# Loads on a second queue, a later transform back and moved weight splits in a one-core kernel: state-space convolution, then an MLP mixer

## The chip, the cores and the metric

The kernel runs on one core of one Trainium2 chip. The metric is the device time of one execution in microseconds (us), the median of three runs. A core has TensorE (PE, products), VectorE (DVE), ScalarE (ACT), GpSimd (Pool) and SyncE (SP). DMAs are issued from SP, ACT or Pool; each of the three has its own queue.

## The reference

Inputs are in fp32; L = 2048 rows, D = 512 channels.

```python
x = A_u
mod = (_silu(c) @ w_mod).reshape(c.shape[0], 6, 1, -1)
sa, ca, ga, sb, cb, gb = ...
h = _layernorm(x) * (1 + ca) + sa
x = x + ga * A_ref(h, ...)       # state-space convolution along L
h = _layernorm(x) * (1 + cb) + sb
x = x + gb * B_ref(h, ...)       # mixer
# A_ref: K[d, l] = Re sum_n C[d,n] exp(dt*A[d,n]*l) dt*B[d,n], l = 0..2047
#        y = irfft(rfft(u, 4096) * rfft(K, 4096))[:2048] + u * Dskip
# B_ref: h  = gelu(layernorm(x) @ w1); its four channel quarters shifted by +1, -1, +2, -2 rows
#        x1 = x + shifted(h) @ w2
#        out = x1 + gelu(layernorm(x1) @ w3) @ w4      # w3 is 512 x 1376
```

## The kernel before, in words

The order on each engine is the order in which the code is written, inside blocks of `tc.manual_schedule()`; tiles come from pools, and a framework puts in the waits. An engine and a DMA queue run their line strictly in order: what stands behind a waiting instruction waits too.

The work has five stages.

1. Up to about 209 us: the convolution kernel K is built (exponentials, sines, products), the normalised input is taken through a first transform and stored to DRAM as VU. During this stage Pool copies w3, w4 and w2 to DRAM scratch (`WD`), in pieces hung on the steps of that loop (`side`).
2. `k_first`: eight rounds of products turn K (tile KX) into VK0 and VK1, one for each half `jh` of 256 channels.
3. Sixteen steps, two halves `jh` of eight `kc`. A step takes the block of VU loaded by `load_vu` (512 KB, a tile of the pool `ldp`, name `ld`), transforms it (`spectrum_u`, ACT copies it to `us`), transforms K (`spectrum_k`), multiplies both on DVE (`multiply`: four products `ma`, `mb` and two sums `zc`), and in the next step transforms back (`back`: PE to PSUM `pz`, ACT copies to `z`, Pool stores z to DRAM as ZT in two DMAs of 256 KB). On ACT, z of the step before stands ahead of `us` of the step after. `flip` makes a sign-changed copy T3 of a part of table T2 on Pool. Table `Gm` belongs to `back`, table `FI` to the inverse.
4. The inverse: `load_inv(jh, k)` reads ZT back (512 KB or halves of it), `inv_half` multiplies with FI on PE, and DVE adds the result to x, which lies in X2, the same memory as KX (`load_x`, four loads of 1 MB). For the first half `jh = 0` the groups g = 0, 3, 1, 2 of four row tiles run during or right after the steps, with `half_stat` on DVE for the statistics; for the second half they run after the gap in which the last z makes its way through DRAM.
5. Mixing and channel groups. Mixing takes the eight tiles t = 7, 0, 1, 2, 3, 4, 5, 6 of 256 rows: modulation and statistics on DVE, normalisation on ACT (`mix_norm`), transposes on PE, then `mix_half(t, hl, hf)`: products with w1, a gelu on ACT into tile `go` (two buffers), and `mix_out` stores `go` to DRAM (GD). Tiles 4 to 6 are mixed inside the channel groups. A channel group g reads four shifted windows of GD (`chan_load`), multiplies with w2 (`chan_sum`), normalises, and runs w3, gelu and w4 (`chan`).

All products of the mixer are in three parts: a value is split into a high part (ACT rounds it to fp32r) and a low part (DVE subtracts), for weights and for the moving data (`nh`, `nl`). `weights` makes the tiles of one weight and a `load` that returns a function `split`. `split_w(n)` runs the next n splits of w3 and w4, each of 512 columns by 128 rows, in the order in which they were loaded.

Of the kernel before, what the change touches and what calls it, by code (L numbers as in the profile page):

```python
# [106 lines left out]
def body(ctx, tc, A):  # L107
# [11 lines left out]
    GD = dpool.tile([4, 128, 20, 128], F32, name="GD")  # L119
    WD = {k: dpool.tile(list(A[k].shape), F32, name="D" + k) for k in ("w2", "w3", "w4")}  # L120

# [425 lines left out]
    with tc.manual_schedule():  # L547
# [49 lines left out]
        for f in later:  # L597
# [8 lines left out]
    TU = TU[0]  # L606
    Gm = c2.tile([128, 2, 64], F32, name="Gm")
# [47 lines left out]

    t3s = {}

    def flip(kc):
        t = t3s[kc] = c2.tile([128, 8, 64], F32, name="T3", bufs=3)
        for gh in range(2):  # L660
            r = slice(gh * 64, gh * 64 + 64)
            P.tensor_scalar(t[r], T2[kc // 4][r, kc % 4 * 4:kc % 4 * 4 + 8, 64 - gh * 64:128 - gh * 64], -1.0, None, op0=OP.mult)

    def spectrum_k(jh, kc):
        p = [kbank([128, 2, 2, 128]) for gh in range(2)]
        for i in range(2):
            for ro in range(2):
                for ri in range(2):
                    for kk in range(2):
                        for gh in range(2):  # L670
                            k1 = kc * 4 + 2 * kk + i
                            rows = slice(gh * 64, gh * 64 + 64)
                            w = T2[k1 // 16][rows, k1 % 16]
                            if ri == gh:
                                w = w[:, ro * 64:ro * 64 + 64]
                            elif ro == ri:
                                w = w[:, gh * 64:gh * 64 + 64]
                            else:
                                w = t3s[kc // 2 * 2][rows, k1 % 8]
                            T.matmul(p[gh][kk * 64:kk * 64 + 64, i, ro], w,  # L680
                                     VK[jh][rows, ri * 32 + k1].rearrange("p j g -> p (j g)"),
                                     start=(ri == 0), stop=(ri == 1), skip_group_check=True)
        return p
# [33 lines left out]
    def load_inv(jh, k, i=None, q=Y):  # L717
        if (jh, k) not in zis:
            zis[jh, k] = block()
# [23 lines left out]
    def weights(pl, src, rows, cols, name, ntile):  # L743
        hi = pl.tile([128, ntile, cols], F32R, name=name + "h")
        lo = pl.tile([128, ntile, cols], F32R, name=name + "l")

        def load(stage, i, m=1, c0=0, c1=cols):
            n = min(128, rows - i * 128)
            w = stage(m, c1 - c0) if stage else lo.bitcast(F32)[:, i:i + m, c0:c1]
            Y.dma_start(w[:n], src[i * 128:i * 128 + (m - 1) * 128 + n, c0:c1].rearrange("(a p) n -> p a n", p=n))  # L750

            def split():
                for j in range(m):
                    h = hi[:n, i + j, c0:c1]
                    act(h, w[:n, j])
                    V.tensor_sub(lo[:n, i + j, c0:c1], w[:n, j], h.bitcast(F32))  # L756
            return split
        return hi, lo, load

    def two(m, n):  # L760
        return block().rearrange("p (a c) b -> p a (c b)", a=2)

# [79 lines left out]

    def mix_w(hl, f2):
        p = psw.tile([128, 2, 256], F32, name="pm")
        for e in range(2):
            three(p[:, e], W1h, W1l, hl, slice((f2 * 2 + e) * 128, (f2 * 2 + e + 1) * 128))
        return p

    def mix_out(g, hf, go):
        Y.dma_start(dram(GD, (2 + 2 * g) * 128 + hf * 256 * 2560, [[2560, 128], [128 * 2560, 2], [1, 256]]), go)  # L850
        if g not in (0, 7):
# [76 lines left out]

    def mix_half(t, hl, hf):
        p = mix_w(hl, hf)  # L930
        go = gop.tile([128, 2, 256], F32, name="go")
        act(go, p, AF.Gelu_apprx_tanh)
        mix_out(t, hf, go)
# [148 lines left out]
    splits = []  # L1082
# [9 lines left out]
    def split_w(n):  # L1092
        for _ in range(n):
            splits.pop(0)()

    steps = [(jh, kc) for jh in range(2) for kc in range(8)]
    with tc.manual_schedule():
        load_vu(*steps[0])
        flip(0)
        Y.dma_start(Gm, A["G"].rearrange("p (a b) -> p a b", a=2))  # L1100
        for r in range(8):
            k_first(r)
            if r == 3:
                load_vu(*steps[1])
            if r == 6:
                load_vu(*steps[2])
        us = spectrum_u(*steps[0])
        split = None
        for n, st in enumerate(steps):
            p = spectrum_k(*st)  # L1110
            multiply(*st, us, p)
            if n == 7:
                v0x.close()
                pw2 = ctx.enter_context(pool("pw2", side="right", reuse_waits="tile"))
                pw1 = ctx.enter_context(pool("pw1", side="right", reuse_waits="tile"))
                W2h, W2l, ldw2 = weights(pw2, WD["w2"], 512, 512, "w2", 4)
                W1h, W1l, ldw1 = weights(pw1, A["w1"], 512, 512, "w1", 4)
            if n > 0:
                back(*steps[n - 1])
            if n == 15:  # L1120
                i1 = inverse_parts(0, 1, psb, "pk2")
# [8 lines left out]
            if n == 9:  # L1130
                Y.dma_start(FI, A["FI"].rearrange("p (a b c) -> p a b c", a=32, b=2))
            if split:
                split()
                split = None
            if n in (8, 9):
                split = ldw1(two, n % 2 * 2, 2)
            if n == 10:
                for k in (0, 3, 4, 7):
                    load_inv(0, k)
            if n == 12:  # L1140
                inverse(0, 0)
                w2s = [ldw2(None, 2 * i, 2) for i in range(2)]
                for b in range(4):
                    half_stat(b, 0)
            if n == 13:
                inverse(0, 3)
                for k in (1, 2, 5, 6):
                    load_inv(0, k)
            if n in (14, 15):
                w2s.pop()()  # L1150
        for f in i1:
            f()
        back(*steps[15])
        s2x.close()
        tp = lambda name, bufs=1, **k: pool(name, bufs, reuse_waits="tile", **k)
        cm = ctx.enter_context(tp("cm", 2, side="right"))
        hv = ctx.enter_context(tp("hv", side="right"))
        gop = ctx.enter_context(tp("gop", 2, side="right"))
        psT = ctx.enter_context(tp("psT", space=PSUM))
        psw = ctx.enter_context(tp("psw", 2, space=PSUM))  # L1160
# [6 lines left out]
        for k, i in ((3, 1), (0, 0)):  # L1167
            load_inv(1, k, i, Y)
            load_inv(1, k + 4, i, S)
        for k, i in ((3, 0), (0, 1)):  # L1170
            load_inv(1, k, i)
            load_inv(1, k + 4, i)
        for i in range(2):
            inv_half(0, 2, i, psy, "py")()
        for b in (14, 15, 4, 5, 6, 7):
            half_stat(b, 0)
        for k in (1, 2):
            load_inv(1, k)
            load_inv(1, k + 4)
        keep(6)  # L1180
        inv_half(1, 3, 1, psy, "py")()
# [48 lines left out]
        load_w3(0)  # L1230
        mix_half(1, hl, 0)
        mix_norm(2)
        first_stats(3)
# [10 lines left out]
        load_w4(2)  # L1244
        mix_half(2, hl, 0)
        chan_split(0)
        mix_norm(3)
# [6 lines left out]
        add1 = chan_sum(0, 1)  # L1254
        split_w(1)
        n = cm.tile([128, 2, 512], F32, name="h2")
# [9 lines left out]
        stat0(0)  # L1266
        split_w(1)
        add1()
        mix_half(3, hl, 0)
        stat0(1)  # L1270
        norm0(0)
        norm0(1)
        split_w(1)
        mix_half(3, hl, 1)
        r = transposed(n)
        split_w(1)
        r = parts_of(r)
        split_w(4)
        chan_add(0)
# [22 lines left out]
```

## Time and profile before

| | us |
|---|---|
| median of three runs (689.29 to 690.67) | 690.18 |
| the profiled execution | 691.26 |
| its span, first to last instruction | 689.5 |

Mean granted TensorE clock 0.989. In the profile an instruction is named by its line, its engine, what it writes and what it reads (`zc<-ma`). `L115` is the helper `act`, through which all of ACT's copies and functions go. In a row of the timeline stand the start, the duration and, in brackets, the idle time ahead of it and who ended it. Rows of the waits read: engine, tile and line that waited, `<-` who was waited for, total us, times, longest.

### The profile page before, as it was taken

How to read it: one execution, taken by the hardware profiler on the slowest of the kernel's cores; microseconds unless marked ns; L12 is line 12 of the kernel's file. 1: busy time of each engine (PE TensorE's matmuls, PEld its weight loads, DVE VectorE, ACT ScalarE, POOL GpSimd, SP SyncE). 2: the span in 40 equal slices, each digit the busy share in tenths (PEclk: the TensorE clock that was granted, in tenths of full speed). 3: DMA queues.
4: the chain of work that ended last, by engine and by line, in shares of the span. 5: the costliest groups of instructions: out<-in, count | busy, mean ns of one | idle time of the engine just before them, and what ended most of it. 6: DMA issues, size and time to landing. Idle time of an engine off the chain costs nothing.

```text
span 689.5 us, 16884 instructions
## 1 busy us (share of the span) xinstructions
PE 642.6 (93%) x7195; PEld 509.2 (74%) x7195; DVE 498.0 (72%) x795; ACT 331.2 (48%) x505; POOL 124.8 (18%) x236
## 2 busy tenths in 40 slices
PE   1899999999999998977998999999999999999996
PEld 0456655655569776634887889999899889898895
DVE  7899999999996887986987967464574536363522
ACT  3878988889875557432444623123131312222121
POOL 4011112112103355413741101001010000000000
PEclk9999999999999999998999999999999999999999
DMA  8603264643739997967387010020100201010001
GB/s 299 284 2 79 75 218 105 209 121 85 275 85 317 354 335 258 346 204 226 108 257 240 1 32 32 16 77 15 47 31 17 77 1 62 1 49 13 1 31 31
DMA packets 51091, 86.42 MB, mean 125 GB/s; under 512 B 4676, under 2 KB 39496, under 8 KB 48424
## 3 DMA queue, kind: packets, MB, share of 16 engines
q1 hardware_dynamic: 46712, 66.74, 30.1%
q0 software_dynamic: 3440, 17.57, 7.4%
q8 instruction: 56, 0.92, 0.6%
q10 hardware_dynamic: 864, 1.05, 0.5%
q14 instruction: 19, 0.16, 0.1%
HBM read 59.12 MB, written 32.90 MB: 133 GB/s over the span
## 4 chain that ended last, share of the span: by engine, by line
PE 70%; DVE 6%; DMA 5%; ACT 3%; POOL 2%; issue 1%; ACTq 0%; SPq 0%; DVEq 0%; POOLq 0%
PE pm L841 7%; PE pm L838 7%; PE pm L839 7%; PE xx L448 7%; PE pa L954 6%; PE pa L955 6%; PE pa L962 6%; PE kp L498 3%; DMA ZT<-z 3%; PE ph L893 2%; PE ph L895 2%; PE ph L892 2%; DMA ld<-ZT 2%; PE pu L426 2%; PE pT L803 2%; PE pk L626 2%
## 5 line engine op out<-in xcount | busy, mean ns | idle before, releaser
L115 ACT ACTIVATE gh<-pm 128x512 fp32r<-128x512 f32 (+1 forms) x48 | 26.9, 560 | 200.7 <-PE pm L841 200.7
L838 PE MATMUL pm<-nh,w3h 128*128 128x256 f32 (+1 forms) x352 | 86.6, 281 | 2.7 <-ACT nh L115 2.7
L839 PE MATMUL pm<-nh,w3l 128*128 128x256 f32 (+1 forms) x352 | 86.3, 280 | 0.1
L946 DVE TENSOR_TENSOR gl<-gf,gh 128x512 fp32r<-128x512 f32 (+1 forms) x48 | 30.8, 643 | 68.4 <-ACT gf L115 68.4
L954 PE MATMUL pa<-w4h,gh 128*128 128x512 f32 (+1 forms) x176 | 69.6, 395 | 0.0
L838 PEld LDWEIGHTS pm<-nh,w3h 128*128 128x128 f32 (+1 forms) x352 | 66.0, 187 | 4.4 <-ACT nh L115 2.9
L955 PE MATMUL pa<-w4l,gh 128*128 128x512 f32 (+1 forms) x176 | 68.9, 392 | 0.0
L839 PEld LDWEIGHTS pm<-nh,w3l 128*128 128x128 f32 (+1 forms) x352 | 65.9, 187 | 2.2 <-DVE w3l L756 0.5
L765 POOL TENSOR_TENSOR rs<-mv,eps_t 128x1 f32<-128x1 f32 (+1 forms) x39 | 11.0, 282 | 282.4 <-DVE mv L771 265.4
L841 PE MATMUL pm<-nl,w3h 128*128 128x256 f32 (+1 forms) x352 | 55.0, 278 | 0.0
L449 PE MATMUL xx<-MG,ON 64*128 64x512 f32 x160 | 48.1, 397 | 0.0
L962 PE MATMUL pa<-w4h,gl 128*128 128x512 f32 (+1 forms) x176 | 48.0, 390 | 0.0
L448 PE MATMUL xx<-MG,ON 64*128 64x512 f32 x160 | 48.0, 396 | 0.0
L841 PEld LDWEIGHTS pm<-nl,w3h 128*128 128x128 f32 (+1 forms) x352 | 47.0, 187 | 0.0
L898 DVE TENSOR_TENSOR h<-h,ph 128x512 f32<-128x512 f32 x16 | 11.0, 687 | 45.1 <-PE ph L895 45.1
L466 DVE SCALAR_TENSOR_TENSOR e<-tr,p 128x512 f32<-128x512 f32 x64 | 41.1, 684 | 1.5 <-ACT tr L115 1.5
L498 PEld LDWEIGHTS kp<-e,e 128*32 128x32 f32 x2048 | 30.1, 110 | 12.7 <-issue 7.6
L475 DVE TENSOR_TENSOR e<-tr,p 128x1024 f32<-128x1024 f32 x32 | 39.0, 1220 | 0.0
L476 DVE TENSOR_TENSOR e<-tr,m 128x1024 f32<-128x1024 f32 x32 | 39.0, 1219 | 0.0
L115 ACT ACTIVATE p<-xx 128x1024 f32<-128x1024 f32 (+1 forms) x40 | 37.5, 979 | 2.2 <-PE xx L252 1.0
L962 PEld LDWEIGHTS pa<-w4h,gl 128*128 128x128 f32 (+1 forms) x176 | 33.0, 188 | 7.3 <-DVE gl L946 0.2
L115 ACT ACTIVATE tr<-xx 128x1024 f32<-128x1024 f32 x32 | 33.0, 1030 | 9.6 <-PE xx L449 7.9
(236 smaller groups left out, 1731.6 us busy)
## 6 DMA issues: line engine op xcount, KB each, us to landing
VU<-vs SPq DMA_DIRECT2D x64, 128.0 KB, 3.7
ld<-VU SPq DMA_DIRECT2D x16, 512.0 KB, 7.4
ZT<-z POOLq DMA_DIRECT2D x30, 256.0 KB, 6.2
ld<-ZT SPq DMA_DIRECT2D x12, 512.0 KB
Dw<-in_w POOLq DMA_DIRECT2D x8, 688.0 KB, 4.7
xu<-in_u SPq DMA_DIRECT2D x4, 1024.0 KB, 8.0
KX<-in_x SPq DMA_DIRECT2D x4, 1024.0 KB, 8.0
GD<-go SPq DMA_DIRECT2D x16, 256.0 KB, 2.3
```

Source lines behind the costliest of these rows:

```text
L115: return S.activation(out, in_, f, bias=bias, scale=scale)
L448: T.matmul(x[:, :512], la, ma, start=(i == 0), stop=(i == len(ops) - 1))
L449: T.matmul(x[:, 512:], lb, mb, start=(i == 0), stop=(i == len(ops) - 1))
L466: V.scalar_tensor_tensor(e0[:, 1, a], tr[:, 1, 0], 1.0 - 2.0 * a, mg[:, a], op0=OP.mult, op1=OP.mult)
L475: V.tensor_mul(e0[:, 0], tr[:, 0, 0:1].to_broadcast([128, 2, 512]), mg)
L498: T.matmul(kp[32 * j:32 * j + 32, (k % 2) * 4 + g], e1[:, r, d], e0[:, r, :, d * 32:d * 32 + 32], start=(r == 0), stop=(r == 1), skip_grou ...
L838: T.matmul(p, wh[:, k, c], hi[k], start=(k == 0), stop=False)
L839: T.matmul(p, wl[:, k, c], hi[k], start=False, stop=False)
L841: T.matmul(p, wh[:, k, c], lo[k], start=False, stop=(k == 3))
L954: T.matmul(acc[i], gh[:m, e, s], W4h[:m, f], start=(f == 0), stop=False)
L955: T.matmul(acc[i], gh[:m, e, s], W4l[:m, f], start=False, stop=False)
L962: T.matmul(acc[i], gl[:m, e, s], W4h[:m, f], start=False, stop=(f == 10))
```

## The change

- **Loads in the steps.** `load_x` is issued by Pool, one load after the multiply of steps 0, 2, 4 and 6, in the order of the groups 0, 3, 1, 2; it was issued by SP in steps 3, 4, 6 and 8. VU blocks are asked for four steps ahead instead of three, from a pool of six buffers instead of seven. FI is loaded during `k_first`, Gm behind it into the memory of FK. `z` has three buffers instead of two.
- **Flips.** T3 is one tile for the whole table, made once ahead of the steps by eight Pool instructions; before, two instructions stood in every second step, and all of them were done again for the second half.
- **w1** is copied to DRAM scratch in stage 1 like w2, loaded from there by Pool in steps 8 and 9 straight into its low tile, split by ACT in steps 13 and 14, and subtracted by DVE only in the gap. `split` now does ACT's part and returns DVE's part as a function.
- **Transform back of the first half.** The early inverse of groups 0 and 3 moves from steps 12 and 13 to 14 and 15; the four blocks of it come from a pool of their own (`zi`), the other four from `ldp` at step 12. The inverse of group 1 moves from step 15 behind the last `back`.
- **w2** is loaded behind the inverse loads of the second half; ACT splits it behind the first gelu of tile 1, DVE subtracts behind the first gelu of tile 2.
- **Gelu stores** of tiles 2 and 3 are issued by Pool instead of SP. The two inverse loads that ACT issued in the gap are issued by SP.
- **Order into the channel groups.** Statistics and normalisation of group 0 stand ahead of mix_half(3, 0); the transposes of its n stand between the two products of mix_half(3, 1); the splits move with them.

```diff
-    WD = {k: ... for k in ("w2", "w3", "w4")}
+    WD = {k: ... for k in ("w1", "w2", "w3", "w4")}
...
-        side[28 + 3 * k].append(lambda i=k * 256: P.dma_start(WD["w2"][i:i + 256], A["w2"][i:i + 256]))
+        for j, w in enumerate(("w1", "w2")):
+            side[24 + 4 * j + 2 * k].append(lambda w=w, i=k * 256: P.dma_start(WD[w][i:i + 256], A[w][i:i + 256]))
...
-    ldp = a2.enter_context(pool("ldp", bufs=7))
+    ldp = a2.enter_context(pool("ldp", bufs=6))
...
-        z = s2.tile([128, 4, 256], F32, name="z")
+        z = s2.tile([128, 4, 256], F32, name="z", bufs=3)
...
-        Y.dma_start(X2[:, g * 4:g * 4 + 4].rearrange("p b d -> p (b d)"), A["x"][g])
+        P.dma_start(X2[:, g * 4:g * 4 + 4].rearrange("p b d -> p (b d)"), A["x"][g])
...
             def split():
                 for j in range(m):
-                    h = hi[:n, i + j, c0:c1]
-                    act(h, w[:n, j])
-                    V.tensor_sub(lo[:n, i + j, c0:c1], w[:n, j], h.bitcast(F32))
+                    act(hi[:n, i + j, c0:c1], w[:n, j])
+
+                def low():
+                    for j in range(m):
+                        V.tensor_sub(lo[:n, i + j, c0:c1], w[:n, j], hi[:n, i + j, c0:c1].bitcast(F32))
+                return low
...
     def mix_out(g, hf, go):
-        Y.dma_start(dram(GD, ...), go)
+        q = P if g in (2, 3) else Y
+        q.dma_start(dram(GD, ...), go)
...
-            if n + 3 < 16:
-                load_vu(*steps[n + 3])
-            if n % 2 == 0 and n < 14:
-                flip(steps[n + 2][1])
-            if n in (3, 4, 6, 8):
-                load_x(n - 3 if n < 5 else n // 2 - 1)
+            if n + 4 < 16:
+                load_vu(*steps[n + 4])
+            if n in (0, 2, 4, 6):
+                load_x((0, 3, 1, 2)[n // 2])
...
-            if n == 12:
+            if n == 14:
                 inverse(0, 0)
-                w2s = [ldw2(None, 2 * i, 2) for i in range(2)]
                 for b in range(4):
                     half_stat(b, 0)
-            if n == 13:
+            if n == 15:
                 inverse(0, 3)
...
         mix_half(1, hl, 0)
+        w2s = w2s()
         mix_norm(2)
...
         mix_half(2, hl, 0)
+        w2s()
         chan_split(0)
...
+        mix_half(3, hl, 1, turn0)
```

Pool's line in the steps, before. The names are the profile's: ZT is the store of z, T the flipped table, KX the load of x, w1l the load of w1.

```order
L706 DMA ZT_61<-z 32x2x1024 x4
L662 TENSOR_SCALAR T_3646<-xu 64x512 x2
L706 DMA ZT_61<-z 32x2x1024 x4
L662 TENSOR_SCALAR T_3792<-xu 64x512 x2
L706 DMA ZT_61<-z 32x2x1024 x4
L662 TENSOR_SCALAR T_3949<-xu 64x512 x2
```

The same place now:

```order
L706 DMA ZT_61<-z 32x2x1024 x4
L724 DMA KX<-in_x 128x2048
L706 DMA ZT_61<-z 32x2x1024 x4
L724 DMA KX<-in_x 128x2048
L706 DMA ZT_61<-z 32x2x1024 x4
L724 DMA KX<-in_x 128x2048
L706 DMA ZT_61<-z 32x2x1024 x4
L750 DMA w1l<-Dw_64 128x2x512
```

The flips have left Pool's line in the steps, and a load stands in it after every second step's stores.

ACT's line in the mixing, from the first gelu of tile 1 (go) to the copies of tile 2's transposes (nh), before; h is the normalisation of tile 2.

```order
L115 ACTIVATE go<-pm 128x512
L115 ACTIVATE h_4980<-h_4980,nm,rs 128x512 x2
L115 ACTIVATE go<-pm 128x512
L115 ACTIVATE nh_5153<-pT_5143 128x512
L115 ACTIVATE nh_5154<-pT_5144 128x512
```

And now:

```order
L115 ACTIVATE go<-pm 128x512
L115 ACTIVATE w2h<-w2l 128x512 x4
L115 ACTIVATE h_4961<-h_4961,nm,rs 128x512 x2
L115 ACTIVATE go<-pm 128x512
L115 ACTIVATE nh_5138<-pT_5128 128x512
L115 ACTIVATE nh_5139<-pT_5129 128x512
```

The four halves of w2 stand between the gelu and the normalisation.

ACT's line at the entry into the channel groups, before: nh of tile 3, then the two gelus of tile 3, then nh of group 0, then its first gelu (gh).

```order
L115 ACTIVATE nh_5275<-pT_5265 128x512
L115 ACTIVATE w3h<-w3l 128x512 x2
L115 ACTIVATE go<-pm 128x512
L115 ACTIVATE w3h<-w3l 128x512
L115 ACTIVATE go<-pm 128x512
L115 ACTIVATE w3h<-w3l 128x512
L115 ACTIVATE nh_5387<-pT_5375 128x512
L115 ACTIVATE nh_5388<-pT_5376 128x512
L115 ACTIVATE w4h<-w4l 128x512 x4
L115 ACTIVATE gh<-pm 128x512
```

And now:

```order
L115 ACTIVATE nh_5264<-pT_5254 128x512
L115 ACTIVATE w3h<-w3l 128x512 x4
L115 ACTIVATE go<-pm 128x512
L115 ACTIVATE w4h<-w4l 128x512 x2
L115 ACTIVATE nh_5365<-pT_5355 128x512
L115 ACTIVATE nh_5366<-pT_5356 128x512
L115 ACTIVATE go<-pm 128x512
L115 ACTIVATE w4h<-w4l 128x512 x2
L115 ACTIVATE gh<-pm 128x512
```

All four w3 halves stand ahead of the first gelu, and nh of group 0 ahead of the second.

More of the change, by code (lines that the diff above doesn't have):

```diff
@@ L119, in body @@
     GD = dpool.tile([4, 128, 20, 128], F32, name="GD")
[L120 removed]
+    WD = {k: dpool.tile(list(A[k].shape), F32, name="D" + k) for k in ("w1", "w2", "w3", "w4")}
     ident = glob.tile([128, 128], F32, name="ident")
@@ L654, in spectrum_u, with flip @@
         return us
[L656 to L662, printed above, removed]
+    T3 = s2.tile([128, 32, 64], F32, name="T3", bufs=1)
+    def flip(i):
+        for a in range(0, 16, 8):
+            for gh in range(2):
+                r = slice(gh * 64, gh * 64 + 64)
+                P.tensor_scalar(T3[r, i * 16 + a:i * 16 + a + 8], T2[i][r, a:a + 8, 64 - gh * 64:128 - gh * 64], -1.0, None, op0=OP.mult)
     def spectrum_k(jh, kc):
@@ L718, in load_inv @@
         if (jh, k) not in zis:
-            zis[jh, k] = block()
+            zis[jh, k] = block() if jh or k in (1, 2, 5, 6) else zip_.tile([128, 4, 256], F32, name="zi")
         a, n = (0, 4) if i is None else (2 * i, 2)
@@ L1099, in body @@
         flip(0)
-        Y.dma_start(Gm, A["G"].rearrange("p (a b) -> p a b", a=2))
+        flip(1)
         for r in range(8):
             k_first(r)
-            if r == 3:
-                load_vu(*steps[1])
+            if r in (1, 3, 5):
+                load_vu(*steps[r // 2 + 1])
             if r == 6:
-                load_vu(*steps[2])
+                Y.dma_start(FI, A["FI"].rearrange("p (a b c) -> p a b c", a=32, b=2))
+        Gm = pa12.tile([128, 2, 64], F32, name="FK")
+        Y.dma_start(Gm, A["G"].rearrange("p (a b) -> p a b", a=2))
         us = spectrum_u(*steps[0])
-        split = None
+        w1s = []
         for n, st in enumerate(steps):
@@ L1172, in body @@
             load_inv(1, k + 4, i)
+        for f in i1:
+            f()
         for i in range(2):
@@ L1176, in body @@
             half_stat(b, 0)
+        for f in w1s:
+            f()
         for k in (1, 2):
```

73 lines of the change are left out of this document (34 added, 39 removed).

## The prediction

> **What bounds the kernel now.** I read the page first, then the busy time by stretch, the waits inside the stretches where TensorE (PE) is not full, and the single instructions around each wait.
>
> ```profile
> span 689.5 us, 16884 instructions
> PE 642.6 (93%) x7195; PEld 509.2 (74%) x7195; DVE 498.0 (72%) x795; ACT 331.2 (48%) x505; POOL 124.8 (18%) x236
> ```
> ```profile
> core 0: us, PE busy (x) PEld busy (x) DVE busy (x) ACT busy (x) POOL busy (x), PEclk, DMA share, GB/s
> 0.00:205.00 205.00, 183.02 (x2892) 112.19 (x2892) 194.20 (x278) 169.21 (x208) 35.62 (x64) 0.99 0.49 153
> 227.30:302.10 74.80, 67.65 (x1420) 49.44 (x1415) 66.71 (x111) 42.65 (x83) 35.15 (x42) 1.00 0.92 313
> 302.10:313.60 11.50, 4.75 (x46) 2.07 (x42) 5.60 (x12) 1.09 (x2) 0.00 (x0) 0.95 0.64 187
> 313.60:371.70 58.10, 55.88 (x454) 46.41 (x454) 47.57 (x93) 20.97 (x32) 28.13 (x76) 0.95 0.64 210
> 371.70:377.30 5.60, 2.93 (x13) 2.93 (x14) 4.13 (x7) 5.17 (x10) 0.00 (x0) 0.70 0.63 185
> 377.30:683.00 305.70, 305.58 (x1961) 275.68 (x1961) 163.83 (x273) 80.67 (x150) 19.90 (x50) 1.00 0.09 28
> ```
>
> The columns are the stretch, its length, busy time of PE, weight loads, DVE, ACT and Pool, then clock, DMA share and GB/s. From 377.3 us on PE is never free (305.58 of 305.70), and the change leaves that work alone. So the end moves one for one with the start of the first channel group. Before it lie three places with slack, and the change works at all three: the sixteen steps (227.3 to 302.1, with the DMA engines at 0.92), the gap in which PE waits for the second half's transform (302.1 to 313.6), and the entry into the channel groups (371.7 to 377.3, clock 0.70). The stage up to 205 us is bounded by DVE; two more DRAM copies of 512 KB there meet a DMA share of 0.49 and cost nothing, unless the VU stores become late.
>
> **The steps.** DVE's groups inside the steps, and who else waits there:
>
> ```profile
> L690 DVE TENSOR_TENSOR ma<-pk,us 128x512 f32<-128x512 f32 x32 | 21.9, 684 | 8.9 <-ACT us L115 5.9 <-PE pk L680 2.6 <-issue 0.5
> L756 DVE TENSOR_TENSOR w1l<-ld,w1h 128x512 fp32r<-128x512 f32 x4 | 3.0, 788 | 1.0 <-ACT w1h L115 1.0
> L734 DVE TENSOR_TENSOR KX<-pz,KX 128x512 f32<-128x512 f32 x4 | 2.6, 685 | 0.0
> L756 DVE TENSOR_TENSOR w2l<-w2l,w2h 128x512 fp32r<-128x512 f32 x3 | 2.0, 689 | 0.3 <-ACT w2h L115 0.3
> L784 DVE BATCH_NORM_STATS2 st<-KX 128x6 f32<-128x256 f32 x4 | 1.4, 416 | 0.0
> ```
> ```profile
> ACT z L115 <- DMA ZT<-z: 8.7, 3, 4.3
> PE pk L680 <- POOL T L662: 1.6, 3, 0.5
> ```
> ```profile
> 261.09 1.09 ACT L115 ACTIVATE z<-pz 128x512 f32<-128x512 f32 x2 [4.34 <-DMA ZT<-z]
> ```
> ```profile
> ld<-VU SPq DMA_DIRECT2D x16, 512.0 KB, 7.4
> ZT<-z POOLq DMA_DIRECT2D x30, 256.0 KB, 6.2
> KX<-in_x SPq DMA_DIRECT2D x4, 1024.0 KB, 8.0
> KX<-in_wm SPq DMA_DIRECT2D x3, 1024.0 KB, 12.1
> ```
> ```profile
> 227.31 0.69 DVE L690 TENSOR_TENSOR ma<-pk,us 128x512 f32<-128x512 f32 x1 [2.12 <-PE pk L680]
> 238.42 0.69 DVE L690 TENSOR_TENSOR ma<-pk,us 128x512 f32<-128x512 f32 x1
> ```
> ```profile
> 300.76 0.69 DVE L692 TENSOR_TENSOR zc<-ma 128x512 f32<-128x512 f32 x1
> 301.36 0.69 DVE L692 TENSOR_TENSOR zc<-mb 128x512 f32<-128x512 f32 x1
> ```
> ```profile
> 240.00:250.00 10.00, 8.63 (x170) 5.63 (x166) 6.81 (x12) 5.11 (x10) 5.38 (x7) 1.00 1.00 367
> ```
>
> The path: SP runs ahead as far as seven buffers let it and fills the DMA engines; the stores of z come late; with two z buffers ACT stops (8.7 us); `us`, behind z on ACT, is late; DVE stops (5.9 us). From the first `ma` (227.31) to the end of the last `zc` (302.05) are 74.7 us, of which DVE is idle 8.9 + 1.0 + 0.3 = 10.2, so 64.5 are work. A step is six operations, which start 0.60 us apart (301.36 - 300.76), so 3.6 us; sixteen are 57.6.
>
> What the change takes from DVE before the last `zc`: four w1 and two w2 subtractions, and two of the four adds of the early inverse, which now stand behind the last multiply. What stays is 57.6 + two adds at 0.60 + four statistics (1.4) = 60.2. Work removed: 64.5 - 60.2 = 4.3 us.
>
> What is left of the 10.2 us of idle time I bound from both sides. Below: the first steps run without a stall and start (238.42 - 227.31) / 3 = 3.70 apart, 0.1 over DVE's own 3.6, so 15 x 0.1 = 1.5 is left when no DMA is late (Pool's sign flips, gone from the steps, were part of it). Above: everything that is removed comes back as waiting, 10.2 + 4.3 = 14.5. What decides is bytes. In the first half two steps now move two VU loads, four half stores and one x load, six times 0.52 MB = 3.15 MB; at the 367 GB/s of the full stretch above this is 8.6 us against 2 x 3.70 = 7.4. With four x loads the deficit is 4 x 1.2 = 4.8. The second half moves 4.2 MB of inverse loads, 1.05 of w1, 3.7 of stores and 1 of VU, 9.9 MB or 27 us, against 7 x 3.7 + 2.6 = 28.5: it fits. So I take 1.5 + 4.5 = 6.0 us of idle time; the third z buffer and six loaded VU blocks absorb a little of the deficit. Gain in the steps: 4.3 + 10.2 - 6.0 = 8.5 us; ends 13.0 and 0.
>
> ```profile
> 209.31 6.20 POOL L662 TENSOR_SCALAR T<-xu 64x512 f32<-64x512 f32 x4 [26.16 <-DMA wm<-in_TU]
> 223.37 1.06 PE L626 MATMUL pk<-FK,KX 64*128 64x128 f32 x16
> ```
>
> The Pool queue holds x, w1 and z in one line now. Behind each x stands the next z store; behind the flips stands the first x, but eight flips end some 12.4 us after 209.3, and PE reads KX until 224.4, so the x isn't held up by them. On SP the small Gm load waits for PE's last k_first and holds VU blocks 4 and 5 back until then; they are needed about three steps later. The w1 halves of ACT (four) fall in steps 13 and 14, behind `us`, as w2's did.
>
> **The gap.**
>
> ```profile
> 303.26 1.09 ACT L115 ACTIVATE z<-pz 128x512 f32<-128x512 f32 x2 [2.91 <-PE pz L702]
> ```
> ```profile
> 313.63 2.81 PE L731 MATMUL py<-ld,FI 128*32 128x256 f32 x21 [6.45 <-DMA ld<-ZT]
> ```
>
> From the last `zc` it takes 313.63 - 302.05 = 11.6 us until the stored z has come back. The other work put there (first-half inverse adds, four w1 subtractions, some 8 us of DVE) fits beside it. Two things lie on the path: the last back transform shares two PSUM banks with the inverse of group 3, whose adds now stand behind the last `zc`, one or two adds of 0.60 us, and I take 0.7; and two loads move from ACT's queue to SP's, 0.4 us each to issue, ahead of 1 MB that takes longer, so 0 (up to 0.8). With six blocks instead of seven one more load waits for a buffer; it is due only at the third inverse: 0, up to 0.5.
>
> **The mixing.** The w2 split moves behind the gelu of tile 1.
>
> ```profile
> 299.20 1.15 ACT L115 ACTIVATE w2h<-w2l 128x512 fp32r<-128x512 f32 x2
> ```
> ```profile
> 348.54 1.72 ACT L115 ACTIVATE h<-h,nm,rs 128x512 f32<-128x512 f32 x2
> ```
> ```profile
> 350.57 1.03 PE L803 MATMUL pT<-ident,h 128*128 128x128 f32 x8
> ```
> ```profile
> 357.91 1.22 DVE L879 TENSOR_TENSOR win<-win,wh 128x1024 fp32r<-128x1024 f32 x1 [2.46 <-ACT wh L115]
> ```
>
> Four halves at 1.15 / 2 are 2.3 us on ACT, and queued behind them is the normalisation of tile 2, ready at 348.54 and ended at 350.26, 0.3 before PE wants it. It ends at 352.4 now, and PE, which has nothing else in its line, stands 1.7 us (bounds 0 and 2.3). The four low subtractions, 2.4 us, fit into DVE's wait of 2.46 ahead of the window split. The load itself goes out in the gap's shadow.
>
> **The entry.**
>
> ```profile
> 365.93 0.88 SPq L850 DMA_DIRECT2D GD<-go  x2
> ```
> ```profile
> 371.71 0.60 ACT L115 ACTIVATE go<-pm 128x512 f32<-128x512 f32 x1 [7.66 <-PE pT L803]
> ```
> ```profile
> 374.37 0.58 PE L838 MATMUL pm<-nh,w3h 128*128 128x256 f32 x1 [2.69 <-ACT nh L115]
> ```
> ```profile
> 372.86 0.69 DVE L756 TENSOR_TENSOR w3l<-w3l,w3h 128x512 fp32r<-128x512 f32 x1 [3.78 <-ACT w3h L115]
> ```
> ```profile
> 374.30:377.30 3.00, 2.93 (x13) 2.93 (x14) 3.00 (x6) 2.58 (x6) 0.00 (x0) 0.50 0.91 251
> ```
>
> The gelu of tile 3 writes a buffer whose last store (tile 2) stood on SP behind fifteen weight loads until 365.93. ACT stops 7.66 us; behind it stand two w3 halves and the transposed n; PE stops 2.69 us and then runs 3.0 us at half clock, some 13 products of 0.21 us where 0.12 is usual: 1.4. Now Pool issues the store as soon as the gelu ends; with the 6.2 us of the z stores it lands before 365. And n is transposed between the two products of tile 3, so that ACT's copy runs under 1.4 us of PE work. DVE, idle for 3.78 us there today, fills this time with the five subtractions put ahead of n's low part (3.0 us). Gain 2.7 + 1.4 = 4.1, bounds 0 and 4.6.
>
> [...]
>
> **The sum.** -8.5 (steps) + 0.7 (gap) + 1.7 (mixing) - 4.1 (entry) = -10.2 us. The profiled execution took 691.26 us for its span of 689.5 and stands 1.1 above the median of 690.18, so the shift is put on the median: 680.0.
>
> **The rivals.**
> (a) The DMA engines keep the steps where they are: every wait that goes returns. For it speaks the share of 0.92, against it that 227 to 302 moved 313 GB/s and full stretches 367. Time: 690.2 + 0.7 + 1.7 - 4.1 = 688.5. [...] The trace agrees that the engines are nearly full, but not that they were busy with what was due next.
> (b) The steps reach their floor, 1.5 us idle: 680.0 - 4.5 = 675.5.
> (c) The stores on Pool land no earlier, because fifteen weight loads are in flight beside them: the entry stays as it is, 684.1. Against it: the z stores share the engines with loads too and land in 6.2.
> (d) Slower: x and z in one line. A store behind an x lands after 8.0 + 6.2 = 14.2 us, three z buffers cover 3 x 3.7 = 11.1, so four x loads cost 12.4 and the steps end at 227.3 + 61.7 + 12.4 = 301.4, hardly earlier. If x takes the 12.1 us of the slowest loads above, it is 4 x 7.2 = 28.8: the steps end at 317.8, and the time is 704. It decides against the change where each x delays z by more than 3.7 us. Against it: x goes out when z is two steps away, and its share of the engines is larger with SP held to one block a step.
>
> **How the numbers follow.** Forecast 0.56 (677 to 685 by itself), (a) 0.16, (b) 0.14, (c) 0.06, (d) 0.08. Within 0.2% (1.4 us) is what a measurement of this kernel cannot tell from no change: that is 688.8 to 691.6. (a) lies at its edge; I give it 0.10 to faster and 0.06 to same. Faster 0.86, same 0.06, slower 0.08. The range takes in (b) and (a): 674 to 689.
>
> **What would show it.** In the profile after: the last `zc` near 293.5 and DVE's idle time ahead of `ma` near 6 us, ACT's wait of z on its store below 4; the first transform product some 12 us after it; PE idle 1 to 2 us ahead of the transposes of tile 2; no idle time and a full clock at the first w3 product. It is wrong if ACT's z still waits for ZT stores as long as before, above all in steps 2 to 8 behind x, or if VU blocks come late.

## The result, and the profile after

The changed kernel took 681.49 us in the median (680.54 to 683.44, six runs), the kernel before beside it 689.39 us (687.31 to 690.67, six runs): a ratio of 0.9888 with a 95% interval of 0.9868 to 0.9909, so 7.7 us faster (6.3 to 9.1). The profiled execution of the changed kernel took 680.79 us; that of the kernel before (691.26) was one of its slower ones, so the two traces lie 10.5 us apart and the medians 7.9. The account below is one between the traces.

The busy time by stretch, of the changed kernel, with the columns of the prediction's table:

```profile
span 679.0 us, 16871 instructions
PE 633.4 (93%) x7195; PEld 506.5 (75%) x7195; DVE 497.4 (73%) x795; ACT 331.4 (49%) x505; POOL 120.1 (18%) x240
```
```profile
226.40:294.30 67.90, 61.03 (x1384) 48.39 (x1379) 61.01 (x103) 40.60 (x79) 19.39 (x35) 1.00 0.95 327
294.30:309.00 14.70, 8.32 (x94) 4.04 (x98) 8.29 (x16) 1.09 (x2) 0.00 (x0) 0.93 0.67 202
309.00:364.00 55.00, 50.40 (x425) 42.37 (x418) 49.99 (x97) 24.98 (x40) 30.20 (x79) 0.99 0.66 219
363.00:369.00 6.00, 5.91 (x51) 5.70 (x50) 5.83 (x10) 4.36 (x8) 1.61 (x3) 1.00 0.90 289
```

The steps are 6.9 us shorter (67.9 for 74.8), and the entry into the channel groups runs without idle time at full clock (5.91 busy of 6.00, clock 1.00; before, 0.50 in its worst part). The gap in between has become longer. Timeline rows at its ends:

```profile
293.58 0.68 DVE L692 TENSOR_TENSOR zc<-mb 128x512 f32<-128x512 f32 x1
...
296.69 1.09 ACT L115 ACTIVATE z<-pz 128x512 f32<-128x512 f32 x2 [4.23 <-issue]
...
294.92 1.67 PE L702 MATMUL pz<-zc,FK 64*64 64x512 f32 x6 [0.97 <-DVE KX L734]
...
307.69 3.29 PE L731 MATMUL py<-ld,FI 128*32 128x256 f32 x32 [5.76 <-DMA ld<-ZT]
```

From the end of the last `zc` (294.26) it takes 2.43 us to z (1.21 before) and 13.43 to the first inverse (11.58 before). The third row says why z is late: PE's last transform back waited for an add of group 3 (`KX`, L734) in the same PSUM banks.

Inside the steps the waits have changed their kind. ACT now waits for PE alone; the wait of z on its store is gone. DVE's idle time is there, but it is PE that is late, and nearly all of PE's own waits have no releaser:

```profile
ACT z L115 <- PE pz L702: 24.0, 15, 2.8
...
PE pk L680 <- issue: 4.9, 5, 1.5
```
```profile
L690 DVE TENSOR_TENSOR ma<-pk,us 128x512 f32<-128x512 f32 x32 | 21.9, 684 | 9.0 <-PE pk L680 9.0
```

Of the 9.0 us, 2.11 stand ahead of the very first `ma`; 6.9 fall into the steps. "issue" is time in which an engine waited for nothing that the profile shows. The stops stand here:

```profile
248.57 0.33 PE L680 MATMUL pk<-VK,xu 64*64 64x128 f32 x3 [0.59 <-issue]
...
254.96 1.09 PE L650 MATMUL pk<-ld,wm 64*64 64x256 f32 x16 [0.39 <-issue]
...
261.31 0.27 PE L680 MATMUL pk<-VK,T 64*64 64x128 f32 x1 [1.15 <-issue]
...
267.64 0.38 PE L680 MATMUL pk<-VK,xu 64*64 64x128 f32 x2 [1.54 <-issue]
...
273.92 0.27 PE L680 MATMUL pk<-VK,T 64*64 64x128 f32 x1 [0.31 <-issue]
...
280.07 0.27 PE L680 MATMUL pk<-VK,T 64*64 64x128 f32 x1 [1.36 <-issue]
```
```profile
261.31:267.64 6.33, 4.79 (x127) 3.93 (x127) 5.15 (x9) 2.56 (x5) 2.56 (x4) 1.00 1.05 371
267.64:273.92 6.28, 5.97 (x126) 4.69 (x126) 4.84 (x8) 4.08 (x9) 1.21 (x3) 1.00 0.96 299
250.00:260.00 10.00, 9.61 (x222) 7.65 (x215) 9.13 (x16) 6.49 (x13) 2.73 (x5) 1.00 1.04 400
```
```profile
q8 instruction: 56, 0.92, 0.6%
```

They come every 6.15 to 6.4 us, in the middle of unrelated products, and between two of them lie 126 or 127 products and as many weight loads, some 254 instructions. The DMA queue "instruction" moved 56 packets of 0.92 MB / 56 = 16.4 KB, for 7195 products and 7195 weight loads: 257 to a packet. So PE stops where a new block of its code begins. The six stops make 5.3 us. In the trace of the kernel before, none of that size stands in the steps.

The trace also holds the start of each packet of this queue. The changed kernel's six stops end 2.33, 2.38, 2.62, 2.50, 2.37 and 2.36 us after the last such packet started. In the changed kernel and the nine experiments with stops it is 2.2 to 2.6 us for each of the 41 stops over 0.25 us. So PE goes on an almost fixed time after a packet of its code starts: it waits for code. With the DMA share at 0.95 over the steps, a block cost up to 1.54 us.

### The profile page after: what moved, and what is told of

The parts are those of the page before. It is cut to its first block, busy times and chain, and to the rows that moved or that the text cites. A ratio compares the mean times of both kernels' runs of the same rounds, so it can differ in the third digit from the quotient of the medians.

```text
span 679.0 us, 16871 instructions
## 1 busy us (share of the span) xinstructions
PE 633.4 (93%) x7195; PEld 506.5 (75%) x7195; DVE 497.4 (73%) x795; ACT 331.4 (49%) x505; POOL 120.1 (18%) x240
## 4 chain that ended last, share of the span: by engine, by line
PE 77%; DVE 5%; ACT 2%; issue 2%; POOL 1%; DMA 1%; SPq 0%; DVEq 0%; ACTq 0%; POOLq 0%
PE pm L841 8%; PE pm L838 8%; PE pm L839 8%; PE xx L448 7%; PE pa L957 6%; PE pa L958 6%; PE pa L965 6%; PE kp L498 4%; PE pk L680 4%; PE ph L895 2%; PE ph L896 2%; PE ph L898 2%; PE pk L626 2%; PE pu L426 2%; PE pz L702 2%
## 5 line engine op out<-in xcount | busy, mean ns | idle before, releaser
L765 POOL TENSOR_TENSOR rs<-mv,eps_t 128x1 f32<-128x1 f32 (+1 forms) x39 | 11.3, 291 | 274.7 <-DVE mv L771 257.3
L498 PEld LDWEIGHTS kp<-e,e 128*32 128x32 f32 x2048 | 30.1, 110 | 12.7 <-issue 8.6
## 6 DMA issues: line engine op xcount, KB each, us to landing
ld<-ZT SPq DMA_DIRECT2D x8, 512.0 KB, 10.5
```

What stands on the lines that cost most here:

```text
L498: T.matmul(kp[32 * j:32 * j + 32, (k % 2) * 4 + g], e1[:, r, d], e0[:, r, :, d * 32:d * 32 + 32], start=(r == 0), stop=(r == 1), skip_grou ...
```

## The experiments

Two numbers are given for most: the ratio to the kernel before on the same chip, and from the trace the time from the third `ma` to the end of the last `zc` (after this called the steps: 71.1 us before, 64.25 changed). The changed kernel itself has the ratio 0.9888 (0.9868 to 0.9909), from another chip. "Stops" are PE's waits in the steps that no releaser explains, over 0.25 us, summed from the trace.

| kernel | median, us | ratio (95%) | steps, us | stops, us | last zc to first inverse |
|---|---|---|---|---|---|
| changed | 681.49 | 0.9888 (0.9868-0.9909) | 64.25 | 5.3 | 13.4 |
| entry_only | 684.94 | 0.9933 (0.9913-0.9952) | 71.5 | 0 | 11.3 |
| pool_stores_only | 687.77 | 0.9978 (0.9963-0.9992) | 71.4 | 0 | 11.1 |
| w2_behind_nh | 679.62 | 0.9859 (0.9842-0.9875) | 63.7 | 4.6 | 13.5 |
| inv3_other_banks | 679.67 | 0.9853 (0.9834-0.9871) | 63.1 | 4.1 | 12.35 |
| no_x_loads | 677.12 | 0.9827 (0.980-0.9854) | 60.3 | 1.2 | 14.9 |
| z_two_buffers | 683.99 | 0.9929 (0.9907-0.9952) | 65.9 | 2.2 | 14.2 |
| w1_low_in_steps | 683.38 | 0.9923 (0.9895-0.9951) | 65.6 | 3.9 | 14.5 |
| x_on_sp | 680.03 | 0.9865 (0.9842-0.9888) | 63.3 | 4.0 | 13.25 |
| combined | 679.22 | 0.9853 (0.9828-0.9877) | 63.4 | 4.3 | 12.4 |
| combined_x_late | 677.11 | 0.9819 (0.980-0.9839) | 61.3 | 2.4 | 13.1 |
| half_spectrum | 676.18 | 0.982 (0.9787-0.9854) | 59.5 | 0 | 14.2 |
| combined_act_loads | 675.64 | 0.9822 (0.9803-0.9842) | 61.1 | 1.9 | 12.7 |

**The entry by itself.** The kernel before, with the Pool stores and the new order (`mix_w`, `mix_half` and the code behind `transposed(mh.pop(3)[0])` as in the change):

```diff
+        q = P if g in (2, 3) else Y
+        q.dma_start(dram(GD, ...), go)
...
+        mix_half(3, hl, 1, turn0)
```

> The kernel before with one part of the change: the gelu stores of tiles 2 and 3 on Pool and the new order into the channel groups. Theory (the parts add up, and the entry gave 3.8 us in the profiles): 4.0 us faster than before, no PE idle time and a full clock at the first w3 product. Rival (the store lands no earlier beside the fifteen weight loads; the gain of the whole change comes from the steps): within 1 us of before, and ACT still waits some 7 us for the store of tile 2.

It was 4.6 us faster (3.3 to 6.0), and the entry had neither idle time nor half clock. In its profile, the stretch from PE's last products of tile 3 on:

```profile
366.30:372.30 6.00, 5.91 (x49) 5.66 (x48) 5.74 (x10) 4.36 (x8) 1.70 (x3) 1.00 0.86 278
```

**The Pool stores alone**, in the old order:

> The kernel before with the two Pool stores alone, in the old order. Theory: ACT's stop at the gelu of tile 3 goes, and with it most of PE's 2.69 us of idle time and the half clock, 3 to 4 us faster; the new order is worth less than 1 us. Rival (the order does it): under 1.5 us faster, PE idle over 1.5 us at the first w3 product, because n is still transposed behind both products of tile 3.

It was 1.5 us faster (0.6 to 2.6): less than the theory's 3 to 4 us and at the edge of the rival's, but the idle time at the first w3 product is 0.51 us, not the rival's 1.5. Two rows of its timeline show what the order adds:

```profile
373.39 0.38 PE L838 MATMUL pm<-nh,w3h 128*128 128x256 f32 x1 [0.51 <-ACT nh L115]
...
382.08 0.74 PE L963 MATMUL pa<-w4h,gl 128*128 128x512 f32 x2 [0.81 <-DVE gl L947]
```

The store removes most of the 2.69 us at the first w3 product, 0.51 is left; but DVE is late at the first low part of the gelu, 0.81 us. In the new order both stops are gone. So the two parts belong together. By the times about a third of the entry's gain is the queue's (1.5 of 4.6 us), by the traces about half: from the transposed tile 3 to the end of the span it takes 327.6 us before, 325.5 with the Pool stores and 323.3 with the new order too.

**The w2 split in a better place.**

```diff
         mix_half(1, hl, 0)
-        w2s = w2s()
         mix_norm(2)
...
         load_w4(2)
+        w2s = w2s()
         mix_half(2, hl, 0)
```

> The changed kernel with ACT's part of the w2 split moved from ahead of the normalisation of tile 2 to behind the transposed high part of tile 2, where ACT is idle for 2.9 us ahead of the gelu. Theory (the split delays the normalisation, the transposes and all of PE's line): 0.8 us faster than the changed kernel, PE idle ahead of the transposes of tile 2 back from 1.0 to 0.3 us. Rival (the place only moves the delay: 2.2 us of ACT work ahead of the gelu make the window's split late): no faster, and PE waits for the window split instead.

The ratio lies 0.003 lower, and the intervals overlap, so the times alone don't tell it. The traces do. In the changed kernel PE waits twice for the normalisation behind the split; in the experiment only the 0.35 us of the kernel before is left, and the split (2.20 us) lies in ACT's idle time:

```profile
345.67 0.44 PE L803 MATMUL pT<-ident,h 128*128 128x128 f32 x2 [0.76 <-ACT h L115]
346.38 0.87 PE L803 MATMUL pT<-ident,h 128*128 128x128 f32 x6 [0.27 <-ACT h L115]
```
```profile
345.56 0.39 PE L838 MATMUL pm<-nh,w1h 128*128 128x256 f32 x1 [0.35 <-ACT nh L115]
```
```profile
345.87 2.20 ACT L115 ACTIVATE w2h<-w2l 128x512 fp32r<-128x512 f32 x4
349.52 0.60 ACT L115 ACTIVATE go<-pm 128x512 f32<-128x512 f32 x1 [1.45 <-issue]
```

From the first gelu of tile 1 to that of tile 2 it took 349.52 - 341.65 = 7.87 us, for 8.62 in the changed kernel and 7.86 in the kernel before. So the split's old place costs 0.75 us.

**The banks of the gap.**

```diff
             if n == 15:
-                inverse(0, 3)
+                for f in inverse_parts(0, 3, psb, "pk2"):
+                    f()
```

> The changed kernel with the inverse of group 3 in the PSUM banks of the spectrum (four of them) instead of those of the last transform back. Theory (the last transform back waits for the adds of group 3 in the same banks): z starts 1.2 us after the last zc instead of 2.4, and the time is 1.0 to 1.2 us under the changed kernel. Rival (what the gap waits for is the DMA of the second half's loads, which are late for other reasons): z starts earlier, but the first inverse still starts 13.4 us after the last zc, and the time is the same.

```profile
293.76 1.09 ACT L115 ACTIVATE z<-pz 128x512 f32<-128x512 f32 x2 [3.02 <-issue]
...
304.90 1.51 PE L731 MATMUL py<-ld,FI 128*32 128x256 f32 x12 [5.88 <-DMA ld<-ZT]
```

The last `zc` ended at 292.55: z starts 1.21 us later, as in the kernel before, and the first inverse 12.35 later, 1.1 less than in the changed kernel. The gap hands the gain on. By the ratios the run is 2.4 us faster, more than the gap explains, but the intervals just overlap; the trace prices the banks at 1.1. The other 0.8 against the kernel before (11.58) is elsewhere, see the last experiment.

**Without the x loads**, so x is left out of the sum:

```diff
-            if n in (0, 2, 4, 6):
-                load_x((0, 3, 1, 2)[n // 2])
```

> The changed kernel without the four loads of x (4.2 MB) in the steps; X2 keeps old values, so x is left out of the sum. Theory (with the DMA engines full, PE's code comes late: in the changed kernel PE stops six times for nothing the profile shows, 126 to 127 products apart, 5.3 us in all): with 4.2 MB less of some 22 the stops shrink to under 2 us and the steps become 4 to 5 us shorter than the changed kernel's 64.3 us from the third product ma to the end of the last zc. Rival (the stops are a fixed cost of a code block in this stretch, or stand for something else): the stops stay at 4 us or more and the steps stay within 1.5 us.

```profile
PE pk L680 <- issue: 0.6, 1, 0.6
PE pk L650 <- issue: 0.5, 1, 0.5
```
```profile
230.80:291.10 60.30, 58.12 (x1304) 46.85 (x1300) 57.31 (x98) 39.02 (x76) 17.61 (x32) 1.00 0.91 294
```

The steps take 60.3 us, 4.0 less, and the stops fall from 5.3 to 1.15; the gap gives 1.5 back (14.9 us). So the stops are no fixed cost of a code block; they depend on what else the DMA engines move (294 GB/s here, 325 over the same stretch of the changed kernel).

**Fewer PE instructions at the same DMA load.** Only the first of two accumulated products of K's spectrum is made; half of that sum is left out:

```diff
-                for ri in range(2):
+                for ri in range(1):
...
-                                     start=(ri == 0), stop=(ri == 1), ...
+                                     start=True, stop=True, ...
```

> The changed kernel with only the first of the two accumulated products in the spectrum of K (32 products and 32 weight loads a step fewer, of some 176), so half of that sum is left out; all DMAs and all of DVE's work stay. Theory (a block of PE's code takes 6.3 us to come while the DMA engines are full, and a step eats 0.69 of a block): a step eats 0.44 of a block, a block lasts 8.5 us at DVE's pace, the stops go to under 1 us, and from the third ma to the end of the last zc it takes 59.5 to 61 us instead of 64.3. Rival (it is the data that the full DMA engines bring late, VU or room for z): 63 us or more, with DVE waiting for VU blocks or ACT for the stores.

```profile
L690 DVE TENSOR_TENSOR ma<-pk,us 128x512 f32<-128x512 f32 x28 | 19.6, 700 | 0.0
```
```profile
228.20:287.70 59.50, 51.07 (x856) 37.33 (x852) 56.70 (x98) 38.91 (x76) 19.32 (x35) 1.00 0.99 357
```
```profile
PE pz L731 <- DMA zi<-ZT: 3.1, 1, 3.1
```

With the DMA engines fuller than in the changed kernel (0.99, 357 GB/s), DVE has no idle time ahead of `ma` at all, and PE makes no unexplained stop. What the data bring late in the steps is one place only, the loads of the early inverse (3.1 us). So in the changed kernel it was not VU, x or z that came late, but PE. This run also takes products away from PE, and so doesn't by itself tell PE's code from PE's work; that the lost time stood in stops at block borders, each ending an almost fixed time after a packet of code started, is what tells them apart. In the changed kernel it takes 3.7 to 4.0 us from the end of a stop to the start of the next packet, and 2.3 to 2.6 from there until PE goes on, though the packet itself took some 1.0 us. What holds it back stays open.

**Two z buffers instead of three.**

```diff
-        z = s2.tile([128, 4, 256], F32, name="z", bufs=3)
+        z = s2.tile([128, 4, 256], F32, name="z")
```

> The changed kernel with two buffers for z instead of three. Theory (the third buffer is what took ACT's wait for the ZT stores away, 8.7 us in the kernel before, none in the changed one): ACT waits again, 3 us or more, and the time is 2 to 5 us longer than the changed kernel's. Rival (the DMA engines set the pace of the steps in either case, the late stores and the late code only change places): within 1 us.

```profile
ACT z L115 <- DMA ZT<-z: 15.0, 6, 3.5
```

The ratio is 0.9929, some 2.8 us over the changed kernel's, in the range of the theory at its lower end; the two intervals just overlap. The traces have 1.65 us more in the steps and 0.75 in the gap. ACT waits again, longer than in the kernel before (15.0 for 8.7), and the stops shrink to 2.2 us: the rival is partly right too, since one wait takes the place of another.

**The w1 subtractions back in the steps.**

```diff
-                w1s[n - 13] = w1s[n - 13]()
+                w1s.pop(0)()()
...
-        for f in w1s:
-            f()
```

> The changed kernel with DVE's four w1 subtractions back in steps 13 and 14 instead of in the gap. Theory (DVE is without idle time in the last steps, and the gap hides them): the end of the last zc moves out by 4 x 0.60 = 2.4 us and the time with it. Rival (the steps are held by DMA or by PE, and DVE's work there is covered): under 1 us.

The ratio is 0.9923, 2.4 us over the changed kernel's as the theory said, but the intervals overlap, and the trace gives another reason. The last `zc` comes only 1.4 us later (65.6 us), because the stops shrink by 1.4 (5.3 to 3.9) and hide a part of DVE's work. The other 1.05 stands in the gap (14.5), where z came 3.3 us after the last `zc`:

```profile
297.07 2.56 PE L702 MATMUL pz<-zc,FK 64*64 64x512 f32 x8 [1.79 <-DVE KX L734]
```
```profile
297.00:299.70 2.70, 2.62 (x12) 0.61 (x16) 0.62 (x2) 0.00 (x0) 0.00 (x0) 0.64 0.17 50
```

After 1.79 us of waiting the granted clock fell, to 0.64 in this stretch, and the last transform back took 2.56 us for 1.67 in the changed kernel. So DVE's work ahead of the last `zc` counts, but not one for one.

**x on SP.**

```diff
-        P.dma_start(X2[:, g * 4:g * 4 + 4]...
+        Y.dma_start(X2[:, g * 4:g * 4 + 4]...
```

> The changed kernel with the x loads issued by SP at the same steps 0, 2, 4 and 6 instead of by Pool. [...] Rival (on Pool x takes turns with z and is paced by it; on SP it takes turns with the VU loads, which come late): VU blocks land later, PE waits for them, 2 to 4 us slower.

0.9865, where I had put it within 1 us of the changed kernel (0.9888): the same as that kernel, or a little faster. What Pool's queue was to do for x isn't seen. The stops are still there, and move forward: four of five stand between 237 and 257 us, and SP issues the four x loads from 223 to 240 us where Pool did so from 220 to 253.

**A version that beats both.** First the three edits together (w2 behind nh, group 3 in the spectrum's banks, x from SP):

> The changed kernel with three edits that did not cost anything by themselves: ACT's w2 split behind the transposed high part of tile 2, the inverse of group 3 in the banks of the spectrum, x loads from SP. Theory (the three act at three places one behind the other, and add up): the sum of the two that the profiles price, 0.8 + 1.2 us, and 0 to 1.6 for x, so 2 to 4 us faster than the changed kernel. Rival (an earlier z only waits longer for its loads, and the gap gives it back): under 1 us faster.

0.9853, 2.4 us under the changed kernel by the ratios, but no better than the single edits had been. Its trace has all three: z 1.21 us after the last `zc`, 7.84 us from gelu to gelu, and steps of 63.4 us. So the shares of the single edits can't be told by their times. Then the loads of x for groups 1 and 2 later:

```diff
-            if n in (0, 2, 4, 6):
-                load_x((0, 3, 1, 2)[n // 2])
+            if n in (0, 4):
+                load_x(3 * n // 4)
...
+            if n == 13:
+                load_x(1)
+                load_x(2)
```

> The combined kernel with the x loads of groups 1 and 2 (2.1 MB) asked for in step 13 instead of steps 2 and 6, so that they land where the DMA engines are less full (the changed kernel moved 184 GB/s from 286 to 294 us). Theory (full DMA engines make PE's code late between 245 and 282 us; leaving out all four x loads took 4.0 us off the steps): PE's unexplained stops shrink to about half, 1 to 2 us faster than the combined kernel. Rival (the late loads delay the last stores and the second half's loads in the gap): the gap grows by as much, no faster or slower.

```profile
PE pk L650 <- issue: 1.2, 1, 1.2
PE pk L680 <- issue: 1.1, 1, 1.1
```
```profile
250.00:260.00 10.00, 10.00 (x226) 8.19 (x221) 9.63 (x17) 6.21 (x13) 2.33 (x5) 1.00 0.86 254
...
290.00:300.00 10.00, 8.02 (x94) 3.50 (x85) 7.50 (x15) 1.08 (x2) 1.07 (x2) 1.00 0.76 289
```

Nothing is left out here, the 2.1 MB are only moved out of the fullest stretch (254 GB/s from 250 to 260 us, where the changed kernel moved 400). The stops halve (4.3 to 2.4), the steps lose 2.1 us, the gap gives 0.7 back. 677.11 us, 0.9819 (0.980 to 0.9839): clear of the changed kernel's interval, though not of the combined kernel's (0.9828 to 0.9877). Last, two loads of the gap on ACT's queue again:

```diff
-            load_inv(1, k + 4, i, Y)
+            load_inv(1, k + 4, i, S)
```

> The kernel combined_x_late with the two inverse loads of the gap (and the second pair) issued by ACT's queue again, as in the kernel before. Theory (the change made the first inverse of the second half wait for four loads issued one after the other by SP: from the first issue to the first product it took 6.3 to 6.4 us, against 5.7 in the kernel before): the gap from the last zc to the first inverse shrinks by 0.6 us or so, and the time by 0.4 to 0.8 us, hardly to be told from no change in the times. Rival (the loads are bound by bytes): the gap stays.

```profile
296.94 4.56 SPq L721 DMA_DIRECT2D ld<-ZT  x8
```
```profile
302.65 1.94 PE L731 MATMUL py<-ld,FI 128*32 128x256 f32 x16 [6.25 <-DMA ld<-ZT]
```

From the first issue to the first product it takes 302.65 - 296.94 = 5.71 us, as in the kernel before (313.63 - 307.94 = 5.69), for 6.3 with SP alone. The gap is 0.4 us shorter; the ratio, 0.9822 (0.9803 to 0.9842), doesn't tell it from the one above. So the best versions stand 12 us under the kernel before and some 4.7 under the changed one.

## Why the prediction was right, and where it was not

The forecast of 680.0 met 681.49, and each of the places went the way it was said. The four places of the sum moved by 8.1 us together, where 10.2 were predicted and the ratio gives 7.7. That the whole shift between the traces (10.5) is so near the forecast is luck, since 2.4 of it stand outside the sum. The account between the traces, in us:

| | predicted | measured |
|---|---|---|
| steps, first ma to last zc | -8.5 | -6.9 |
| gap | +0.7 | +1.85 |
| mixing | +1.7 | +0.75 |
| entry | -4.1 | -3.8 |
| not in the sum | | -2.4 |

**Steps: right in the sum, wrong in the reason of one term.** Of the 4.3 us of work 3.6 went (67.85 - 6.9 of idle time = 60.95, for 64.5). For the idle time I took 1.5 + 4.5 = 6.0, and 6.9 came. But the 4.5 was put on bytes: data that come late at 367 GB/s, seen as a wait of ACT on the stores or of PE on VU. ACT's wait on the stores was to be below 4 us and is nil; PE doesn't wait for VU. Nor is 367 GB/s a ceiling: the changed kernel moved 400 from 250 to 260 us. The step that failed is "what decides is bytes". In place of late data stand PE's stops at the borders of its code blocks: 5.3 us in the changed kernel, 1.2 without the x loads, none with fewer products. That they come near the 4.5 is luck. The 1.5 is no floor either: half_spectrum, where PE has fewer products to make, has 0.0 ahead of `ma`.

**The third buffer and the moved work** were rightly taken as gains: undone one by one they cost about 2.8 and 2.4 us by the ratios, of which the traces have 1.65 and 1.4 in the steps. The other parts of the change in the steps (VU four steps ahead, the flips, the later inverse) were not undone one by one.

**Gap: the mechanism right, the size off.** The shared banks were said to cost one or two adds, 0.7; with the other bank the gap shrinks by 1.1. The loads that moved to SP's queue were costed at 0 (up to 0.8), with the megabyte behind them as cover; the last run shows 0.6, of which the gap keeps 0.4, since the first product needs the very loads that SP issues one behind the other.

**Mixing: the mechanism right, 1.7 was too much.** I took the end of both normalisations as what PE needs. But its transposes start with the first: the row of two, after 0.76 us of waiting, and the row of six, after 0.27. So the slack was that of the first half, about a microsecond more than I had read. The stops of 1.03 us in all were followed by no half clock (clock 1.00 from 345 to 354 us, 0.99 from 309 to 364).

**Entry: as worked out.** 13.00 us from the transposed tile 3 to the first gelu of group 0, for 16.82. By itself it gave 4.6 (3.3 to 6.0). The rows:

```profile
356.87 1.09 ACT L115 ACTIVATE nh<-pT 128x512 fp32r<-128x512 f32 x2 [1.68 <-PE pT L803]
...
363.00 0.60 ACT L115 ACTIVATE go<-pm 128x512 f32<-128x512 f32 x1 [2.97 <-PE pm L841]
...
369.87 0.60 ACT L115 ACTIVATE gh<-pm 128x512 fp32r<-128x512 f32 x1 [1.49 <-PE pm L841]
```

The gelu of tile 3 waits for PE now and no longer for its buffer (7.66 us before).

**Not in the sum:** the first `ma` came 0.9 us earlier, but over the profiles of this study it lies between 224.6 and 228.1 us, whatever was changed, so I put it down to scatter. From the first gelu of group 0 to the end it is 1.6 us less; half of it is named in the last section.

**The rivals.** (a) did not come: full engines (a DMA share of 0.95, for 0.92 before) didn't keep the steps, which lost 6.9 us. The queue that issues x made no difference for the worse when it was SP again (0.9865 for 0.9888), and asking for 2.1 MB of x later took 2.1 us off the steps. The rival misread what the engines' fullness meant for DVE. (d), x ahead of z in one line, did not come: ACT never waited for a store, and the longest of z's stores took 8.2 us from issue to landing (8.9 before), not 14.2. Nor did Pool's queue finish one transfer before it began the next: the packets of the second x start at 240.66 us, the last of the z store ahead of it at 242.40. (b) and (c) are ruled out by the stops and by entry_only.

## What to carry to other kernels

Where an engine stops for nothing that the profile shows, count its instructions between the stops: equal counts (some 254 here), and a code queue whose packets hold as many (257), point to its own code, and so does an almost fixed time from a packet's start to the end of each stop (2.2 to 2.6 us). The remedy is then to move transfers out of the full stretch, nearer to where their data are first needed, which here took 2.1 us off the steps and gave 0.7 of them back in the gap. A short job on a helper engine (the w2 split) belongs where that engine waits anyway, not ahead of a chain that feeds the bound (0.75 us here); the slack to read is that of the first piece the next engine can start on. Work moved behind a deadline still holds its PSUM banks (1.1 us of the gap here), and two loads that a first product needs together are worth two queues (0.6 us from the first issue to the first product here).

## What the runs showed of the hardware

- In the changed kernel PE's code came late where the DMA engines were full (a DMA share of 1.05 and 0.96 in two stretches shown) and PE went through a block of some 254 products and weight loads in 6.15 to 6.4 us, stops included: up to 1.54 us a block, and up to 1.8 in w2_behind_nh. All 41 stops over 0.25 us stand at these borders (2.2 to 2.6 us after a packet started), though not at every one in every kernel (no_x_loads has two, 1.15 us). With some 8.8 us a block (half_spectrum, 59.5 us for 856 products and 852 weight loads, DMA share 0.99) there was no stop.
- The products with w2 in the channel groups are 3 to 4 ns shorter in the changed kernel, with the same shapes; w2's tile comes from another pool there. Rows of before, and then of after:

```profile
L895 PE MATMUL ph<-w2h,win x64: 390/393/404, 360.4 to 641.3; 128*128 128x512 f32 x64
```
```profile
L898 PE MATMUL ph<-w2h,win x64: 388/389/396, 355.3 to 631.2; 128*128 128x512 f32 x64
```

Set against each other instruction by instruction, the starts of these products account for 0.8 us over eight groups. That it is the place in memory was not tested.
- Waits of 0.51 us (pool_stores_only, first w3 product; the products behind it start 0.12 us apart) and of 0.76 and 0.27 us close together (the changed kernel, mixing; clock 1.00 from 345 to 354 us) were not followed by a half clock. The 2.69 us of the kernel before were (0.50 from 374.3 to 377.3 us), and after the 1.79 us of w1_low_in_steps the clock was 0.64 from 297.0 to 299.7 us.
